# Last stage of an attention, slot-routing and squared-ReLU kernel: half 0 of the next g made in a row, products of w_in moved later in the step

## The chip, the cores and the metric

The kernel runs on one core of a Trainium2 chip. The metric is the device time of one execution in microseconds (us), lower is better. Engines are named as in the profile: PE (TensorE), with PEld for its weight loads, ACT (ScalarE), DVE (VectorE), POOL (GpSimd), SP (SyncE, which issues the transfers). Every engine executes its own instructions in the order in which they were written; between engines only semaphores order the work.

## What is computed

Three layers follow one another. The first two are not touched by the change; the third is where it lies.

```python
x = attention(q, k, v)            # 4 x 8 heads, 576 positions, window of 128; x is [2304, 512]
logits = x @ phi                  # soft routing to 8 experts of 4 slots
d = softmax over tokens;  c = softmax over slots
slot_out = relu((d.T @ x)[e] @ w1[e]) @ w2[e]      # 32 slots, 512 wide
x = c @ slot_out                  # [2304, 512], rank 32
h = maximum(x @ w_in, 0)          # w_in [512, 2048]
out = (h * h) @ w_out             # w_out [2048, 512]
```

Since x has rank 32, the kernel multiplies w_in by the 32 slots first (a small matrix M, 16 blocks of 128 columns) and then gets h from M and the routing weights c.

## The kernel before, in words

The last stage walks over 48 **units** (tb, f): tb is one of three blocks of 768 tokens, f one of 16 blocks of 128 hidden columns, in three groups of f (0 to 2, 3 to 7, 8 to 15), for each group all three tb. For one unit, `emit_h` makes h (two matmuls of 384 columns into the PSUM banks "xb" and "B", half 0 and half 1); `emit_relu` (ACT) reads each half into a buffer; `emit_sq` squares it in float32, `emit_hi` squares it once more with rounding to the matmul type, `emit_lo` (DVE) subtracts the two. High and low part together are "g". `emit_g(i, s)`, s from 0 to 5, takes one sixth of unit i's tokens: three matmuls of 512 columns into one PSUM bank. s of 0 to 2 read half 0 of g, s of 3 to 5 half 1. In the last f of a group each `emit_g` also empties its bank (L741 on ACT and L743 on DVE in the first group, L745 or L749 on DVE in the others).

The weights w_in and w_out arrive as 64-bit floats and are converted in the same stage, block by block: `conv1` on POOL (two operations of L601), `conv2` on DVE (L615, L617, L619 for each half: half 0 is w_in and gives `cin`, half 1 is w_out and gives `co`), `conv3` (ACT L633, then a subtraction L634). `emit_M1` (PE L640, ACT L642) and `emit_M2` (PE L646, ACT L648, DVE L649) turn `cin` into block f of M. M1 uses the bank "xb" and M2 the bank "B", the banks of h.

A prologue written out by hand does unit 0 and the conversions of the first blocks. Then a loop of **steps** i = 1 to 47 emits the matmuls of unit i and, among them, everything that makes g of unit i + 1, together with half a conversion (`half_at[i]` names block and half; where the half is 1 the step also has M1, M2 and `conv3`: an **M step** below). Order within an engine is the order of these calls; the loop body before is:

```python
emit_g(i, 0); hb = emit_h(i + 1); emit_relu(i + 1, hb); emit_g(i, 1)
emit_M1(fm, "xb"); emit_sq(i + 1, ...); emit_g(i, 2); emit_M2(fm, "B")
emit_hi(i + 1); emit_lo(i + 1, 0, dve); emit_lo(i + 1, 1, dve)
conv2(ch[0], halves=((ch[1],),)); conv3(fm, dve)
emit_g(i, 3); emit_g(i, 4); emit_g(i, 5)
```

Of the kernel before, what the change touches and what calls it, by code (L numbers as in the profile page):

```python
# [27 lines left out]
def attn_moe_relu2_kernel(ctx: ExitStack, tc: tile.TileContext, z0, q, k, v, vr, phi, w1, w2, w_in, w_out, cst, out):  # L28
    nc = tc.nc
    pe, act, dve, pool, sp = nc.tensor, nc.scalar, nc.vector, nc.gpsimd, nc.sync  # L30
# [9 lines left out]
    def bank(tag, name):  # L40
        return psum[0].tile([128, 512], F32, tag=tag, name=name, bufs=NBUF[tag])
# [41 lines left out]
    def take(shape, dt, name):  # L83
        used[0] += 1
        assert used[0] <= RING
        return ring.tile(shape, dt, tag="w", name=name)

    def pump(free, spare):
        used[0] -= free
        while wq and used[0] < RING - spare:  # L90
            load_next_w()
# [495 lines left out]
    def temp(tag, i, n, w, dt):  # L587
        if tag not in arena:
            arena[tag] = take([128, 2048], dt, f"arena_{tag}")
        i %= n  # L590
        return arena[tag][:, w * i:w * i + w]

    def spare():
        return 5 - len(arena) + 3 - len(psto) + min(2, 8 - made[0])

    def conv1(f):

        t = wt["f", f]
        y = temp("y", f, 2, 1024, I32).rearrange("p (a n) -> p a n", a=2)
        for a in range(2):  # L600
            pool.tensor_scalar(out=y[:, a].bitcast(F32), in0=t[:, a, :, 1].bitcast(F32), scalar1=2.0 ** -112, scalar2=0.0, op0=ALU.mult, op1=ALU.add)  # L601
        yz_t[f] = y

    def conv2(f, hooks=(), halves=((0, 1),)):
        t, y = wt["f", f], yz_t[f]
        if f not in cin:
            cin[f] = temp("cin", f, 4, 512, F32)
            co_t[f] = temp("co", f, 4, 512, F32)
        dst = (cin[f], co_t[f])
        hooks = dict(hooks)  # L610
        for n, a in enumerate(halves):
            for k in range(3):
                for h in a:
                    if k == 0:
                        dve.tensor_scalar(out=y[:, h], in0=y[:, h], scalar1=3, scalar2=0x7FFFFFFF, op0=ALU.logical_shift_left, op1=ALU.bitwise_and)  # L615
                    elif k == 1:
                        dve.scalar_tensor_tensor(out=y[:, h], in0=t[:, h, :, 1], scalar=-0x80000000, in1=y[:, h], op0=ALU.bitwise_and, op1=ALU.bitwise_or)  # L617
                    else:
                        dve.scalar_tensor_tensor(out=dst[h].bitcast(I32), in0=t[:, h, :, 0], scalar=29, in1=y[:, h], op0=ALU.logical_shift_right, op1=ALU.bitwise_or)  # L619
                if (n, k) in hooks:  # L620
                    hooks[n, k]()
        if 1 in halves[-1]:
            wt.pop(("f", f))
            yz_t.pop(f)
            pump(1, spare())

    def conv3(f, eng=pool):
        p = f // 2
        if f % 2 == 0:
            whl[p] = take([128, 2, 2, 512], F32R, "whl")  # L630
            made[0] += 1
        t, c = whl[p], co_t.pop(f)
        act.activation(out=t[:, f % 2, 0], in_=c, func=AF.Copy)  # L633
        eng.tensor_tensor(out=t[:, f % 2, 1], in0=c, in1=t[:, f % 2, 0].bitcast(F32), op=ALU.subtract)  # L634
# [39 lines left out]
    NF = DFF // 128  # L674
# [7 lines left out]
    def emit_h(i):  # L682
        tb, f = units[i]
        hb = []
        for hf in range(2):
            hb.append(bank(("xb", "B")[hf], "h"))
            c0 = TB * tb + HB * hf
            pe.matmul(out=hb[hf][:, 0:HB], lhsT=Mst[:, 128 * f:128 * f + 128], rhs=cst_sb[:, c0:c0 + HB], start=True, stop=True)  # L688
        return hb
# [3 lines left out]
    def emit_relu(i, hb, hfs=(0, 1), cl=slice(0, HB)):  # L693
        if i not in g_t:
            k0 = [(2 * i + hf) % 4 for hf in range(2)]
            g = [hT_flat[:, HB * k:HB * k + HB] for k in k0]
            g_t[i] = [temp("gh%d" % (k // 2), k % 2, 2, 2 * HB, F32R).rearrange("p (a n) -> p a n", a=2) for k in k0]
            lo_t[i] = (g, g_t[i])
        for hf in hfs:
            act.activation(out=rbuf[hf][:, cl], in_=hb[hf][:, cl], func=AF.Relu)  # L700

    def emit_sq(i, eng, hfs=(0, 1), cl=slice(0, HB)):
        g = lo_t[i][0]
        for hf in hfs:
            r = rbuf[hf][:, cl]
            if eng is act:
                act.activation(out=g[hf][:, cl], in_=r, func=AF.Square)  # L707
            else:
                eng.tensor_tensor(out=g[hf][:, cl], in0=r, in1=r, op=ALU.mult)  # L709

    def emit_hi(i, hfs=(0, 1), cl=slice(0, HB)):
        for hf in hfs:
            act.activation(out=lo_t[i][1][hf][:, 0, cl], in_=rbuf[hf][:, cl], func=AF.Square)  # L713

    def emit_lo(i, hf, eng, cl=slice(0, HB)):
        g, gh = lo_t[i]
        eng.tensor_tensor(out=gh[hf][:, 1, cl], in0=g[hf][:, cl], in1=gh[hf][:, 0, cl].bitcast(F32), op=ALU.subtract)  # L717
# [5 lines left out]
    def emit_g(i, s):  # L723
        tb, f = units[i]
        if f in firsts:
            acc_t[s] = bank(atags[s], "acc")
        gh = g_t[i][s // 3]
        c0 = 128 * (s % 3)
        w = whl[f // 2]
        for a, (x, y) in enumerate(((0, 0), (1, 0), (0, 1))):  # L730
            pe.matmul(out=acc_t[s], lhsT=gh[:, x, c0:c0 + 128], rhs=w[:, f % 2, y, :], start=(f in firsts and a == 0), stop=(f in lasts and a == 2))  # L731
        if f not in lasts:
            return
        a = acc_t.pop(s)
        r0, k = TB * tb + 128 * s, 6 * tb + s
        if f == GROUPS[0][-1]:
            if k >= 6 and k % 4 == 2:
                psto.append(take([128, 4, 512], F32, "psum"))
                part.extend(psto[-1][:, j] for j in range(4))
            if s % 2:  # L740
                act.activation(out=part[k], in_=a, func=AF.Copy)  # L741
            else:
                dve.tensor_copy(out=part[k], in_=a)  # L743
        elif f != NF - 1:
            dve.tensor_tensor(out=part[k], in0=a, in1=part[k], op=ALU.add)  # L745
        else:
            cls = (slice(0, 512),) if i < len(units) - 1 or s < 5 else (slice(0, 256), slice(256, 512))
            for cl, eng in zip(cls, (sp, act)):
                dve.tensor_tensor(out=part[k][:, cl], in0=a[:, cl], in1=part[k][:, cl], op=ALU.add)  # L749
                eng.dma_start(out=out[r0:r0 + 128, cl], in_=part[k][:, cl])  # L750
# [6 lines left out]
    hb = emit_h(0)  # L757
# [23 lines left out]
    hb = emit_h(1)  # L781
# [11 lines left out]
    emit_lo(1, 1, pool)  # L793
    emit_g(0, 5)
    emit_M2(2, "B")
    conv1(4)
    conv2(3, halves=((0,),))
    conv3(2)
    g_t.pop(0)

    halves = [(3, 1)] + [(f, a) for f in range(4, NF) for a in range(2)]
    steps = [i for i in range(1, len(units)) if not (units[i][1] in lasts and i > 8)]
    half_at = dict(zip(steps, halves))
    conv1_at = {i - 1: f for i, (f, a) in half_at.items() if a == 0 and f > 4}
    last_conv = max(half_at)
    where = {u: i for i, u in enumerate(units)}
    assert all(i < where[0, f] for i, (f, a) in half_at.items())
    for i in range(1, len(units)):
        tb, f = units[i]
        nxt = i + 1 < len(units)  # L810
        ch = half_at.get(i)
        fm = ch[0] if ch and ch[1] == 1 else None
        if i in conv1_at:
            conv1(conv1_at[i])
        emit_g(i, 0)
        hb = emit_h(i + 1) if nxt else None
        if nxt:
            emit_relu(i + 1, hb)
        emit_g(i, 1)
        if fm is not None:  # L820
            emit_M1(fm, "xb")
        if nxt:
            emit_sq(i + 1, act if i <= last_conv else dve)
        emit_g(i, 2)
        if fm is not None:
            emit_M2(fm, "B")
        if nxt:
            emit_hi(i + 1)
            emit_lo(i + 1, 0, dve)
            emit_lo(i + 1, 1, dve)  # L830
        if ch:
            conv2(ch[0], halves=((ch[1],),))
        if fm is not None:
            conv3(fm, dve)
        for s in range(3, 6):
            emit_g(i, s)
        g_t.pop(i)
        if tb == NT // TB - 1 and f % 2 and f < NF - 1:
            whl.pop(f // 2)
            pump(1, spare())  # L840
# [49 lines left out]
```

## Time and profile before

| | us |
|---|---|
| median of 3 runs (441.91 to 443.17) | 442.53 |
| the profiled execution, as timed | 442.01 |
| its span, first to last instruction | 440.2 |
| from h of unit 2 to h of unit 31 (steps 1 to 29) | 156.11 |
| the last matmuls, after that | 76.03 |

Read it so: the span is 1.8 us shorter than the time of the same execution. The stretch in the fourth line is the part of the last stage that still converts weights; in the fifth nothing is left but h, g and the output.

### The profile page before, as it was taken

To read this page: it belongs to the slowest core of one execution; us is meant where nothing else is said; L and a number is where in the kernel's file an instruction comes from. 1 tells how busy PE (TensorE), PEld (TensorE's weight loads), DVE (VectorE), ACT (ScalarE), POOL (GpSimd) and SP (SyncE) were. 2 spreads that over 40 slices of the span, in tenths; PEclk is the share of its full clock that TensorE was granted. 3 is DMA by queue.
4 is the path that set the end of the run, shared out by engine and by line. 5 is a ranking of instruction groups with operands and counts; after the bars stand their busy time and mean duration, and the time that the engine had idled before them with its cause. 6 is when DMAs were issued, how large, how long until landed. Compare 5 with 4: busy or idle time off the path is not lost. (4 is left out here: it accounts for less than half of the span.)

```text
span 440.2 us, 8019 instructions
## 1 busy us (share of the span) xinstructions
PE 417.0 (95%) x2623; PEld 306.9 (70%) x2623; DVE 290.2 (66%) x962; ACT 239.0 (54%) x759; POOL 91.3 (21%) x189
## 2 busy tenths in 40 slices
PE   6999999999999999978998999999999999999995
PEld 5777768768766533456776677777777788888884
DVE  4877867877866446586775767566686666447444
ACT  4877857867866211354666655565555553434340
POOL 3544435433532010455111111110100000000000
PEclk9999999999999999968999999999999999999999
DMA  7979859856778799995200502020000003003003
GB/s 233 295 284 270 286 201 279 281 167 235 245 244 322 269 413 424 408 410 228 95 2 0 191 1 96 1 98 0 1 0 1 1 25 121 0 0 144 0 1 144
DMA packets 36794, 70.62 MB, mean 160 GB/s; under 512 B 19984, under 2 KB 22160, under 8 KB 32656
## 3 DMA queue, kind: packets, MB, share of 16 engines
q1 hardware_dynamic: 36608, 69.97, 44.9%
q8 instruction: 21, 0.34, 0.3%
q14 instruction: 21, 0.17, 0.1%
q10 hardware_dynamic: 144, 0.13, 0.1%
HBM read 65.37 MB, written 4.72 MB: 159 GB/s over the span
## 5 line engine op out<-in xcount | busy, mean ns | idle before, releaser
L731 PE MATMUL acc<-whl,arena_gh 128*128 128x512 f32 x864 | 222.2, 403 | 4.3 <-DVE arena_gh L717 1.9
L731 PEld LDWEIGHTS acc<-whl,arena_gh 128*128 128x128 f32 x864 | 160.2, 191 | 43.8 <-DVE arena_gh L717 8.5
L188 POOL TENSOR_SCALAR p<-p,st 128x192 f32<-128x192 f32 (+1 forms) x142 | 56.6, 412 | 79.6 <-DVE st L184 24.7
L176 ACT ACTIVATE p<-p,st 128x192 f32<-128x192 f32 (+1 forms) x144 | 61.2, 428 | 6.3 <-DVE st L166 6.3
L159 PE MATMUL s<-kt,zq 128*128 128x192 f32 (+2 forms) x288 | 60.2, 335 | 4.1 <-DMA kt<-in_k_dram 3.4
L700 ACT ACTIVATE acc<-h 128x384 f32<-128x384 f32 (+2 forms) x49 | 23.6, 481 | 66.6 <-PE h L688 33.6
L717 DVE TENSOR_TENSOR arena_gh<-hT,arena_gh 128x384 fp32r<-128x384 f32 (+1 forms) x95 | 48.6, 551 | 15.8 <-ACT arena_gh L713 12.9
L159 PEld LDWEIGHTS s<-kt,zq 128*128 128x128 f32 x288 | 45.5, 198 | 8.9 <-DMA zq<-in_z_dram 4.1
L601 POOL TENSOR_SCALAR arena_y<-f 128x512 f32<-128x512 f32 x32 | 23.0, 724 | 133.8 <-DVE arena_co L619 62.6
L166 DVE CUSTOM_DVE_ANT_0 p<-s,tbl 128x192 f32<-128x192 f32 (+1 forms) x144 | 41.8, 326 | 5.2 <-PE s L159 4.6
L229 DVE COPY ptb<-tq 64x128 f32<-64x128 f32 x128 | 35.3, 280 | 9.4 <-PE tq L209 7.4
L227 ACT ACTIVATE ptb<-tp 128x256 f32<-128x256 f32 (+1 forms) x72 | 25.5, 355 | 14.7 <-PE tp L207 14.5
L709 DVE TENSOR_TENSOR hT<-acc 128x384 f32<-128x384 f32 (+1 forms) x19 | 10.7, 565 | 29.8 <-ACT acc L700 29.8
L633 ACT ACTIVATE whl<-arena_co 128x512 fp32r<-128x512 f32 x16 | 10.1, 632 | 32.7 <-DVE arena_co L619 22.5
L246 PE MATMUL xa<-ptb,vt 128*64 128x256 f32 x192 | 27.6, 396 | 0.0
L176 ACT ACTIVATION_READ_ACCUMULATOR p<-p,st 128x1 f32 x144 | 27.4, 190 | 0.0
L207 PE MATMUL tp<-cs,p 128*128 128x128 f32 x128 | 26.1, 275 | 1.0 <-ACT xT L263 1.0
L688 PE MATMUL h<-cst_sb,Mst 128*128 128x384 f32 x96 | 25.1, 343 | 0.7 <-DVE Mst L649 0.6
L713 ACT ACTIVATE arena_gh<-acc 128x384 fp32r<-128x384 f32 (+2 forms) x49 | 25.3, 516 | 0.1
L617 DVE SCALAR_TENSOR_TENSOR arena_y<-f,arena_y 128x512 int32<-128x512 int32 x32 | 24.5, 765 | 1.1
L713 ACT ACTIVATE arena_gh<-hT 128x384 fp32r<-128x384 f32 x48 | 25.0, 521 | 0.0
L700 ACT ACTIVATE hT<-h 128x384 f32<-128x384 f32 x48 | 23.3, 485 | 0.0
(172 smaller groups left out, 488.7 us busy)
## 6 DMA issues: line engine op xcount, KB each, us to landing
w_w<-in_w_dram SPq DMA_DIRECT2D x32, 1024.0 KB, 6.7
f<-in_w_in_dram SPq DMA_DIRECT2D x16, 512.0 KB, 10.2
f<-in_w_out_dram SPq DMA_DIRECT2D x16, 512.0 KB, 10.2
zq<-in_q_dram SPq DMA_DIRECT2D x30, 144.0 KB, 3.8
kt<-in_k_dram SPq DMA_DIRECT2D x15, 288.0 KB, 4.1
vt<-in_v_dram SPq DMA_DIRECT2D x16, 256.0 KB, 6.5
out_dram<-psum SPq DMA_DIRECT2D x11, 256.0 KB, 2.1
out_dram<-xn_all SPq DMA_DIRECT2D x4, 256.0 KB, 2.0
```

The costliest lines, as they stand in the source:

```text
L159: pe.matmul(out=sb_t[t][:, 256 * i:256 * i + n], lhsT=zq[u % NQ][:, c].rearrange("p a b -> p (a b)"), rhs=kt_t[u][:, 64 * c + 64 - n:64 * ...
L166: dve.tensor_tensor_reduce(out=p, in0=sb_t[t][:, 256 * i:256 * i + n], in1=tbl[:, 192 * pr + 192 - n:192 * pr + 192], scale=-0.125, scalar ...
L176: act.activation(out=p, in_=p, func=AF.Exp, bias=st[:, i:i + 1], scale=-1.0, accum_out=st[:, 2 + i:3 + i])
L188: eng.tensor_scalar(out=p, in0=p, scalar1=st[:, 4 + i:5 + i], scalar2=0.0, op0=ALU.mult, op1=ALU.add)
L207: pe.transpose(A[:, i, :], p, ident)
L227: act.activation(out=dst, in_=src, func=AF.Copy)
L229: dve.tensor_copy(out=dst, in_=src)
L246: pe.matmul(out=xa_t[u][po:po + 64, 128 * j:128 * j + 256], lhsT=v_t[u][:, j, po:po + 64], rhs=pt[:, 0:4, po:po + 64], start=(j == 0), sto ...
L700: act.activation(out=rbuf[hf][:, cl], in_=hb[hf][:, cl], func=AF.Relu)
L713: act.activation(out=lo_t[i][1][hf][:, 0, cl], in_=rbuf[hf][:, cl], func=AF.Square)
L717: eng.tensor_tensor(out=gh[hf][:, 1, cl], in0=g[hf][:, cl], in1=gh[hf][:, 0, cl].bitcast(F32), op=ALU.subtract)
L731: pe.matmul(out=acc_t[s], lhsT=gh[:, x, c0:c0 + 128], rhs=w[:, f % 2, y, :], start=(f in firsts and a == 0), stop=(f in lasts and a == 2))
```

## The change

The first conversions of the prologue for block 3 move into the loop: half 0 of block 3 in step 1, half 1 in step 2, and so on: each later half moves on by one of the steps that have a conversion. There are 13 M steps as before, the first now step 2 (it was 1) and the last step 29 (it was 28). `conv3(2)` subtracts on DVE instead of POOL. Within a step, relu, square and rounded square of half 0 stand in a row on ACT, and those of half 1 after them; on DVE the order becomes low part 0, conversion, low part 1, L649, L634. M1 stands after `emit_g(i, 2)` and M2 after `emit_g(i, 4)`.

```diff
@@ -793,47 +793,51 @@
     emit_lo(1, 1, pool)
     emit_g(0, 5)
     emit_M2(2, "B")
-    conv1(4)
-    conv2(3, halves=((0,),))
-    conv3(2)
+    conv3(2, dve)
     g_t.pop(0)
 
-    halves = [(3, 1)] + [(f, a) for f in range(4, NF) for a in range(2)]
+    halves = [(f, a) for f in range(3, NF) for a in range(2)]
     steps = [i for i in range(1, len(units)) if not (units[i][1] in lasts and i > 8)]
     half_at = dict(zip(steps, halves))
-    conv1_at = {i - 1: f for i, (f, a) in half_at.items() if a == 0 and f > 4}
+    conv1_at = {i - 1: f for i, (f, a) in half_at.items() if a == 0 and f > 3}
     last_conv = max(half_at)
     where = {u: i for i, u in enumerate(units)}
-    assert all(i < where[0, f] for i, (f, a) in half_at.items())
+    assert all(i + 2 <= where[0, f] for i, (f, a) in half_at.items())
     for i in range(1, len(units)):
         tb, f = units[i]
         nxt = i + 1 < len(units)
         ch = half_at.get(i)
         fm = ch[0] if ch and ch[1] == 1 else None
+        sq = act if i <= last_conv else dve
         if i in conv1_at:
             conv1(conv1_at[i])
         emit_g(i, 0)
-        hb = emit_h(i + 1) if nxt else None
         if nxt:
-            emit_relu(i + 1, hb)
+            hb = emit_h(i + 1)
+            emit_relu(i + 1, hb, (0,))
+            emit_sq(i + 1, sq, (0,))
+            emit_hi(i + 1, (0,))
+            emit_lo(i + 1, 0, dve)
         emit_g(i, 1)
+        emit_g(i, 2)
+        if nxt:
+            emit_relu(i + 1, hb, (1,))
         if fm is not None:
             emit_M1(fm, "xb")
         if nxt:
-            emit_sq(i + 1, act if i <= last_conv else dve)
-        emit_g(i, 2)
+            emit_sq(i + 1, sq, (1,))
+            emit_hi(i + 1, (1,))
+        if ch:
+            conv2(ch[0], halves=((ch[1],),))
+        if nxt:
+            emit_lo(i + 1, 1, dve)
+        emit_g(i, 3)
+        emit_g(i, 4)
         if fm is not None:
             emit_M2(fm, "B")
-        if nxt:
-            emit_hi(i + 1)
-            emit_lo(i + 1, 0, dve)
-            emit_lo(i + 1, 1, dve)
-        if ch:
-            conv2(ch[0], halves=((ch[1],),))
+        emit_g(i, 5)
         if fm is not None:
             conv3(fm, dve)
-        for s in range(3, 6):
-            emit_g(i, s)
         g_t.pop(i)
```

## Rows read from the trace of the kernel before

**Rows 1.** The profile's page, parts 1 and 2: busy time and share of the span of each engine, and the clock granted to TensorE in 40 equal slices (9 is full speed).
```profile
PE 417.0 (95%) x2623; PEld 306.9 (70%) x2623; DVE 290.2 (66%) x962; ACT 239.0 (54%) x759; POOL 91.3 (21%) x189
PEclk9999999999999999968999999999999999999999
```

**Rows 2.** Stretches of the span, each from the start of h of one unit to the start of h of another: us of the stretch, then busy us (and instructions) of PE, PEld, DVE, ACT, POOL, then the granted clock, the share of the transfer engines and GB/s. In order: steps 1, 11, 12, 13, 14, 24 and 33, and last steps 1 to 29 together.
```profile
199.86:208.55 8.69, 6.98 (x30) 5.38 (x31) 5.51 (x9) 3.36 (x9) 4.62 (x5) 0.80 0.53 207
...
257.98:263.93 5.95, 5.38 (x31) 4.06 (x30) 3.68 (x8) 3.07 (x8) 0.66 (x1) 1.00 0.01 3
263.93:268.81 4.88, 4.78 (x21) 3.65 (x20) 2.79 (x6) 3.04 (x7) 0.66 (x1) 1.00 0.59 196
268.81:273.46 4.65, 4.65 (x21) 3.65 (x20) 4.55 (x9) 2.52 (x6) 0.67 (x1) 1.00 0.06 22
273.46:278.74 5.28, 5.28 (x31) 4.03 (x30) 3.74 (x8) 3.05 (x8) 0.00 (x0) 1.00 0.00 0
...
324.63:329.91 5.28, 5.28 (x31) 4.03 (x30) 3.74 (x8) 3.06 (x8) 0.00 (x0) 1.00 0.00 0
...
369.47:373.92 4.45, 4.45 (x22) 3.73 (x21) 1.97 (x4) 1.70 (x4) 0.00 (x0) 1.00 0.00 0
...
199.86:355.97 156.11, 147.36 (x710) 112.42 (x711) 105.97 (x191) 90.83 (x221) 18.54 (x26) 0.99 0.13 46
```

**Rows 3.** The waits of PE and of PEld in steps 1 to 29: engine, tile and line, what it waited for, us in total, times, longest.
```profile
PE MX L640 <- DVE arena_cin L619: 6.8, 10, 1.7
...
PEld acc L731 <- DVE arena_gh L717: 5.8, 15, 0.4
```

**Rows 4.** Timeline of PE in step 11 (an M step): start, us, engine and line, operation, count, and in brackets the idle time before it with its releaser. The twelve matmuls of the last row are s of 3 to 5 of this step and s = 0 of the next. The matmuls' ends are modelled, so the starts are read.
```profile
257.98 0.51 PE L688 MATMUL h<-cst_sb,Mst 128*128 128x384 f32 x2
258.33 0.86 PE L731 MATMUL acc<-whl,arena_gh 128*128 128x512 f32 x3
259.76 0.42 PE L640 MATMUL MX<-arena_cin,soT 128*32 128x128 f32 x8 [0.56 <-DVE arena_cin L619]
260.12 0.98 PE L731 MATMUL acc<-whl,arena_gh 128*128 128x512 f32 x3
260.93 0.38 PE L646 MATMUL MY<-ms,cs 128*128 128x128 f32 x2
261.07 3.02 PE L731 MATMUL acc<-whl,arena_gh 128*128 128x512 f32 x12
```

**Rows 5.** Timeline of ACT: first two operations of the prologue, the second of which reads what the first wrote; then from steps 11 and 12 (the conversion L633 is issued in step 11 and stands ahead of step 12's relu).
```profile
195.20 0.49 ACT L700 ACTIVATE acc<-h 128x384 f32<-128x384 f32 x1 [0.80 <-PE h L688]
195.72 0.52 ACT L713 ACTIVATE arena_gh<-acc 128x384 fp32r<-128x384 f32 x1
...
258.42 0.49 ACT L700 ACTIVATE acc<-h 128x384 f32<-128x384 f32 x1 [1.24 <-PE h L688]
...
261.35 0.28 ACT L648 ACTIVATE Mst<-MY 128x128 fp32r<-128x128 f32 x1
...
264.97 0.63 ACT L633 ACTIVATE whl<-arena_co 128x512 fp32r<-128x512 f32 x1 [2.52 <-issue]
265.51 0.47 ACT L700 ACTIVATE acc<-h 128x384 f32<-128x384 f32 x1
...
267.08 0.52 ACT L713 ACTIVATE arena_gh<-acc 128x384 fp32r<-128x384 f32 x1
267.50 0.52 ACT L713 ACTIVATE arena_gh<-hT 128x384 fp32r<-128x384 f32 x1
```

**Rows 6.** Timeline of DVE: one emptying of a bank in step 6, then step 11.
```profile
232.47 0.69 DVE L743 COPY psum<-acc 128x512 f32<-128x512 f32 x1
...
261.66 0.29 DVE L649 TENSOR_TENSOR Mst<-MY,Mst 64x128 fp32r<-64x128 f32 x1 [2.05 <-ACT Mst L648]
262.07 1.03 DVE L717 TENSOR_TENSOR arena_gh<-hT,arena_gh 128x384 fp32r<-128x384 f32 x2
263.02 0.42 DVE L615 TENSOR_SCALAR arena_y<-arena_y 128x512 int32<-128x512 int32 x1
263.48 0.69 DVE L617 SCALAR_TENSOR_TENSOR arena_y<-f,arena_y 128x512 int32<-128x512 int32 x1
264.20 0.69 DVE L619 SCALAR_TENSOR_TENSOR arena_co<-f,arena_y 128x512 int32<-128x512 int32 x1
```

**Rows 7.** Around step 1: a stretch behind its M1 (columns as in rows 2), then timelines of PE, DVE and POOL; the last row is POOL in step 12.
```profile
203.20:206.50 3.30, 3.30 (x13) 2.69 (x10) 0.73 (x2) 2.20 (x6) 1.28 (x2) 0.50 0.35 133
...
202.87 0.43 PE L640 MATMUL MX<-arena_cin,soT 128*32 128x128 f32 x8 [1.71 <-DVE arena_cin L619]
...
194.97 1.65 DVE L617 SCALAR_TENSOR_TENSOR arena_y<-f,arena_y 128x512 int32<-128x512 int32 x1
...
199.83 0.80 DVE L615 TENSOR_SCALAR arena_y<-arena_y 128x512 int32<-128x512 int32 x1
200.67 1.02 DVE L617 SCALAR_TENSOR_TENSOR arena_y<-f,arena_y 128x512 int32<-128x512 int32 x1
201.72 1.01 DVE L619 SCALAR_TENSOR_TENSOR arena_cin<-f,arena_y 128x512 int32<-128x512 int32 x1
...
200.31 1.87 POOL L601 TENSOR_SCALAR arena_y<-f 128x512 f32<-128x512 f32 x2
...
264.97 0.66 POOL L601 TENSOR_SCALAR arena_y<-f 128x512 f32<-128x512 f32 x1 [4.62 <-DVE arena_co L619]
```

## The prediction, made before the result was known

> **What bounds the kernel now.** I read the page first: PE is busy for 95% of the span at nearly full clock, DVE and ACT for much less [rows 1]. So only time in which PE stands, or does the same work at the lower clock, can be won. Next the stretches between the starts of h in consecutive steps [rows 2]. A step that has only h and 18 matmuls takes 4.45 us, and PE has no hole in it: that is the floor. With M1 and M2 and without a wait it takes 5.28 us (steps 14 and 24), so M1 and M2 cost 0.83. But step 11, also an M step, takes 5.95, step 12 4.88 though it has no M1, and step 1 8.69. Steps 1 to 29 take 156.11 us; after them the steps are at the floor, so the change can win nothing there.
>
> The waits name two causes [rows 3]. M1 stands 6.8 us in 10 M steps for `cin`, which DVE converts last. In step 11 the three matmuls of s = 1 start at 258.33 and need 0.68, yet M1 starts at 259.76 [rows 4]. And the weight loads of `emit_g` wait for low parts of g. Why these are late is seen on ACT: in step 12 relu of half 0 starts at 265.51 instead of 0.44 after h (as in step 11, 257.98 to 258.42), because L633 stands ahead of it and itself waits for `co` [rows 4, 5]. The relus, squares and rounded squares of both halves must then all pass before DVE takes low part 0.
>
> Step 1 has both troubles and a third: M1 waits 1.71 us for `cin` of block 3, whose conversions take 0.80, 1.02 and 1.01, and in the stretch behind that wait the granted clock is 0.50, the 1.2 GHz level [rows 7].
>
> **The change, part by part.** I lay one new M step out from its h start (0), with pitches from rows [rows 4 to 6].
>
> *ACT.* Relu 0 at 0.44. Square 0 reads what relu wrote: such a pair is 0.52 apart (195.20 to 195.72), so 0.96. Rounded square 0 follows by 0.42 at 1.38 and ends at 1.90. Relu 1 starts at 1.80. M1 starts behind two groups of 0.68 and h (0.35), at 1.72 plus a small gap, and its copy on ACT is done by about 2.6; square 1 and rounded square 1 end by about 3.6.
>
> *DVE.* Low part 0 starts at 1.90. Two low parts take 0.95 to the next operation, one 0.48: L615 at 2.38, L617 0.46 later at 2.84, L619 0.72 later at 3.56, ending at 4.25. Low part 1 starts at 4.25 and ends at 4.80; L649 starts at 4.73 and ends at 5.02. L634 follows when L633 is done, about 5.7, which is 0.4 into the next step, before that step's low part 0.
>
> *What each consumer needs.* Low part 0 ends at 2.45; s = 0 of the next unit starts at 4.45 - 0.68 = 3.77 or later, so that wait goes, with 1.3 to spare. Low part 1 is needed at 4.45 + 0.35 + 1.37 = 6.17: 1.37 to spare. `cin` is made a step earlier, so M1's wait goes. L633 stands behind rounded square 1 and finds `co` at 4.3, so it ends about 5.0 and the next relu (5.28 + 0.44) is not held. M2's copy on ACT ends before low part 1 does, as M2 to copy takes 0.42.
>
> *The new wait.* L649 reads bank "B", into which half 1 of the next h goes. In an M step of 5.28 that matmul starts at 5.28 + 0.17 = 5.45; L649 ends at 5.02, so 0.43 to spare. In steps 2 and 8 two DVE copies of a bank (s = 2 and 4, 0.69 each) stand ahead of L649 as well: 5.02 + 1.38 = 6.40, a stall of 0.95 each. Behind it stand all later matmuls.
>
> *Cost of M1 and M2 in the new place.* Not shown. From below the gaps from their own start to the next group: 0.36 (259.76 to 260.12) and 0.14 (260.93 to 261.07), 0.50. From above 0.83 as measured. Nothing in the move shortens the switch from and to small matmuls, so I take 0.83.
>
> *Prologue, POOL and DMA.* The first L615 to L619 of block 3 leave the place in front of M1; `conv3(2)` goes to DVE, where an L634 (about 0.7) fits before low part 0 of step 1, 1.90 after h. I cost it at nothing; uncovered it would be those 0.7, once. POOL's first conversion of a block is released as soon as an earlier block's half is done [rows 7], steps before it is used, and stays so. The transfers of w_in and w_out are issued when a block is consumed, with several blocks in the ring, so the shift by a step costs nothing; a late one would hold only POOL. Step 1, without M1 and its wait, then runs at full clock; if the 3.3 us at the lower level stayed, that would add 1.65, as half of it would be lost.
>
> *Emptying at the end of a group.* Step 13, with six of them, takes 4.65, 0.20 over the floor. Between 0 and 0.20 for each of six such steps (2, 5, 8, 13, 18, 23); low part 0 no longer waits behind three of them, so 0.10.
>
> **The sum for steps 1 to 29.** 29 x 4.45 = 129.05; 13 x 0.83 = 10.79; 2 x 0.95 = 1.90; 6 x 0.10 = 0.60; together 142.3. Against 156.11 the gain is 13.8. The profiled execution took 442.01, so 428.2. The median of the runs is 0.5 higher; I forecast 428.5, between the two readings. With M1 and M2 at 0.50 and no stalls the sum is 135.55, gain 20.6: 421.5.
>
> **A rule weighed against a row.** Beside POOL's L601, two of which took 1.87 instead of 2 x 0.66, L615, L617 and L619 took 0.80, 1.02 and 1.01 instead of 0.42, 0.69 and 0.69: both engines got slower, DVE by 1.03 in all [rows 6, 7]. POOL's L601 is released by the end of L619 [rows 7], so in the new order it falls beside low part 1 and L649, where before DVE was idle or done.
>
> The Trainium skill, "SBUF — State Buffer", section "Who interferes with whom", says that DVE and GpSimd contend only for one shared pair of ports, held exclusively for a whole instruction. By that rule the loser would stand still for all of the other's operation; the rows agree that there is contention, but show both longer.
>
> **Rivals.**
> *POOL blocks DVE once per M step.* If low part 1 or L649 stood for a whole L601, 0.66, L649 would end at 5.68, half 1 of h would wait 0.23, and 13 of these cost 3.0: 431.5. For it: the overlap is new. Against: low part 1 has started before L601 is released.
>
> *Conversions stretched as in step 1.* L615 to L619 1.03 longer in every step puts L649 at 6.05; h waits 0.60 in 13 M steps, 7.8: 436. Against: from step 2 on the operations take 0.42, 0.69 and 0.69, since POOL's part comes after them.
>
> *The gap only moves; no change.* Low part 1, now behind the conversion, could hold s = 3 of the next unit. To give back 13.8 in 29 steps it must cost 0.48 each, so be 1.37 + 0.48 = 1.85 later than laid out: 442.5. Against: the worst stretch of a whole conversion in rows is 1.03.
>
> *Slower: L649 holds h.* Its place is bank "B" in every M step. It decides from a delay of 0.43 + 13.8 / 13 = 1.5 us beyond my layout. For it: one L617 beside POOL took 1.65 instead of 0.69, 2.4 times [rows 7]. Were all three stretched so (1.80 to 4.3), L649 would be 2.5 late, the stall 2.1, 13 times 27: 455. Against: that row is from the prologue, beside several POOL operations in a row.
>
> **How the numbers follow.** Forecast 0.64, POOL's blocking 0.11, stretched conversions 0.10, no change 0.07, slower 0.08. Faster 0.85, the same 0.07 (within 0.3%, 1.3 us, about what a measurement of this kernel can tell from no change), slower 0.08. The range runs from the lower bound, 421.5, to the stretched conversions, 436, and leaves out the last two cases and part of the spread about the others.
>
> **What the profile after would show.** The wait of M1 for `cin` gone; the weight loads' wait for low parts near zero; steps without M1 at 4.45 and M steps near 5.28; steps 1 and 2 together about 9.7 where step 1 alone took 8.69, with the clock at 1.00; L633 no longer ahead of relu 0; a new wait of h for L649 of steps 2 and 8. I am wrong if h waits for L649 in all M steps, if low part 1 holds s = 3, or if M steps cost far from 0.83.

## The result, and the profile after

| | before | after |
|---|---|---|
| median of the runs, us | 442.85 (4 runs, 441.91 to 443.52) | 428.85 (4 runs, 428.07 to 429.97) |
| the profiled execution, as timed | 442.01 | 429.43 |
| its span | 440.2 | 427.6 |
| h of unit 2 to h of unit 31 | 156.11 | 141.74 |

The ratio is 0.9687, 95% interval 0.9655 to 0.9719: 14 us faster. The forecast was 428.5.

First the page of the kernel after, parts 1 and 2:

```profile
PE 410.1 (96%) x2623; PEld 306.1 (72%) x2623; DVE 292.7 (68%) x961; ACT 248.7 (58%) x761; POOL 95.0 (22%) x188
PEclk9999999999999999987999999999999999999999
```

Against [rows 1] the same number of matmuls takes 7 us less of PE's busy time. The page alone does not say where the gain is; the stretches from h to h do. The columns are those of [rows 2]; the rows are steps 1, 2, 3, 11, 12 and 13 of the kernel after, and steps 1 to 29 together:

```profile
201.90:206.45 4.55, 4.55 (x21) 3.83 (x21) 3.22 (x6) 3.03 (x7) 2.27 (x4) 1.00 0.97 383
206.45:211.72 5.27, 5.27 (x31) 4.03 (x30) 4.31 (x9) 4.47 (x11) 1.17 (x2) 1.00 0.07 26
211.72:217.10 5.38, 4.72 (x21) 3.66 (x20) 4.35 (x9) 3.27 (x8) 1.42 (x2) 1.00 0.54 195
...
252.49:256.94 4.45, 4.45 (x22) 3.72 (x21) 2.99 (x6) 2.75 (x6) 0.16 (x1) 1.00 0.01 4
256.94:262.21 5.27, 5.27 (x31) 4.03 (x30) 3.50 (x8) 3.77 (x9) 1.63 (x2) 1.00 0.03 5
262.21:266.66 4.45, 4.45 (x21) 3.72 (x20) 3.74 (x7) 2.75 (x6) 0.00 (x0) 1.00 0.66 231
...
201.90:343.64 141.74, 140.42 (x710) 111.99 (x711) 104.51 (x190) 96.70 (x223) 21.94 (x25) 1.00 0.14 51
```

Of the 14.37 us that this stretch got shorter, 7.43 are time in which PE stood (156.11 less 147.36 before, 141.74 less 140.42 after). The other 6.94 had been counted as busy: 1.70 in step 1, the lower clock (6.98 against 5.28 for an M step), and most of the rest in steps like step 12 before, where PE is counted busy for 4.78 [rows 2] with what takes 4.45 when no weight load waits. So a share of busy time of 95% hides a part of what can be won; steps laid beside the floor do not.

The work of DVE, 104.51, is about what it was (105.97), and ACT has 6 us more; PE waits for them in two places only. What is left of waits of PE and PEld in the same stretch, columns as in [rows 3] (the list has beside these only waits of PEld on "issue", for which the profile shows no releaser: 4.6 us at M1 and 2.6 us at `emit_g`):

```profile
PE h L688 <- DVE Mst L649: 1.3, 2, 0.7
...
PEld h L688 <- DVE Mst L649: 2.6, 3, 1.0
```

M1's wait for `cin` and the wait for low parts are gone, and the new wait is the one that was expected, twice. Here it is at the end of step 2 (h start 206.45), on DVE and PE:

```profile
211.65 0.68 DVE L743 COPY siT<-acc 128x512 f32<-128x512 f32 x1
212.37 0.29 DVE L649 TENSOR_TENSOR Mst<-MY,Mst 64x128 fp32r<-64x128 f32 x1
...
212.72 0.44 PE L688 MATMUL h<-cst_sb,Mst 128*128 128x384 f32 x1 [0.66 <-DVE Mst L649]
213.00 4.27 PE L731 MATMUL acc<-whl,arena_gh 128*128 128x512 f32 x18
```

Now step 12, an M step in the new order, on ACT, DVE and POOL, and the next h on PE (its second matmul is 0.17 behind the start shown):

```profile
257.31 0.49 ACT L700 ACTIVATE acc<-h 128x384 f32<-128x384 f32 x1 [1.65 <-PE h L688]
257.83 0.52 ACT L707 ACTIVATE hT<-acc 128x384 f32<-128x384 f32 x1
258.26 0.51 ACT L713 ACTIVATE arena_gh<-acc 128x384 fp32r<-128x384 f32 x1
258.68 0.47 ACT L700 ACTIVATE hT<-h 128x384 f32<-128x384 f32 x1
...
258.81 0.56 DVE L717 TENSOR_TENSOR arena_gh<-hT,arena_gh 128x384 fp32r<-128x384 f32 x1 [1.64 <-ACT arena_gh L713]
259.28 0.42 DVE L615 TENSOR_SCALAR arena_y<-arena_y 128x512 int32<-128x512 int32 x1
...
261.07 0.55 DVE L717 TENSOR_TENSOR arena_gh<-hT,arena_gh 128x384 fp32r<-128x384 f32 x1
...
261.24 0.90 POOL L601 TENSOR_SCALAR arena_y<-f 128x512 f32<-128x512 f32 x1 [3.56 <-DVE arena_co L619]
...
261.65 0.29 DVE L649 TENSOR_TENSOR Mst<-MY,Mst 64x128 fp32r<-64x128 f32 x1
...
262.21 0.50 PE L688 MATMUL h<-cst_sb,Mst 128*128 128x384 f32 x2
```

Counted from its h start, 256.94: relu 0 at 0.37, square 0.89, rounded square 1.32, relu 1 at 1.74, low part 0 at 1.87, L615 at 2.34, low part 1 at 4.13, L649 from 4.71 to 5.00; the next h at 5.27, its half 1 at 5.44. The reader sees 0.44 us between the end of L649 and the matmul that needs its bank. POOL's L601 starts 0.17 behind low part 1 and takes 0.90 where it took 0.66 [rows 7]; low part 1 takes its 0.55.

### The profile page after: what moved, and what is told of

Its sections match the earlier page's. It is cut to its first block, busy times and chain, and to the rows that moved or that the text cites. A ratio compares the mean times of both kernels' runs of the same rounds, so it can differ in the third digit from the quotient of the medians.

```text
span 427.6 us, 7977 instructions
## 1 busy us (share of the span) xinstructions
PE 410.1 (96%) x2623; PEld 306.1 (72%) x2623; DVE 292.7 (68%) x961; ACT 248.7 (58%) x761; POOL 95.0 (22%) x188
## 4 chain that ended last, share of the span: by engine, by line
PE 51%; DVE 2%; ACT 1%; issue 0%; DVEq 0%
PE acc L731 45%; PE h L688 4%; PE MX L640 1%; DVE psum L749 1%; PE MY L646 1%; DVE arena_y L617 1%; DVE arena_y L615 0%; ACT whl L633 0%; DVE arena_gh L717 0%; DVE Mst L649 0%; DVE arena_co L619 0%; ACT siT L741 0%; ACT psum L741 0%; DVEq L890 0%; ACT ms L642 0%
## 5 line engine op out<-in xcount | busy, mean ns | idle before, releaser
L731 PE MATMUL acc<-whl,arena_gh 128*128 128x512 f32 x864 | 214.9, 397 | 2.4 <-DVE arena_gh L717 1.9
L717 DVE TENSOR_TENSOR arena_gh<-hT,arena_gh 128x384 fp32r<-128x384 f32 (+1 forms) x95 | 52.7, 555 | 38.5 <-ACT arena_gh L713 34.1
L601 POOL TENSOR_SCALAR arena_y<-f 128x512 f32<-128x512 f32 x32 | 28.4, 892 | 122.3 <-DVE arena_cin L619 55.1
L688 PEld LDWEIGHTS h<-cst_sb,Mst 128*128 128x128 f32 x96 | 18.2, 191 | 7.7 <-DVE Mst L649 3.8
```

## The experiments

The theory: the gain is PE's holes in all steps, closed by getting DVE to the conversion and to L649 early; what remains is the floor, 0.83 for each M step, and the time by which L649 is late for the next h. The rivals: it is the start with its wait and low clock; it is the late products alone; it is the order of the halves alone. Four kernels take the change apart.

**e1: the start alone**, on the kernel before:

```diff
-    conv1(4)
-    conv2(3, halves=((0,),))
-    conv3(2)
+    conv3(2, dve)
...
-    halves = [(3, 1)] + [(f, a) for f in range(4, NF) for a in range(2)]
+    halves = [(f, a) for f in range(3, NF) for a in range(2)]
...
```

> Only the start of the change: conversions of block 3 leave the prologue, every later half one step on, conv3(2) on DVE; the loop body stays the old one. Theory (PE's holes in all steps are the gain): step 1 falls from 8.69 to an M-less step of about 4.9, step 29 becomes an M step of about 5.95, so the gain is about 2.7 us: 440, and M1 still waits about 6 us in all for cin. Rival (the start with its low clock is most of the gain): 431 to 434.

Measured: 442.15 against 442.81, ratio 0.998 (0.9962 to 0.9998). Steps 1, 12, 13 and 1 to 29, then ACT at the start of step 13 (h start 267.58):

```profile
201.17:205.73 4.56, 4.56 (x20) 3.85 (x21) 2.62 (x5) 2.81 (x7) 2.19 (x3) 1.00 0.94 370
261.63:267.58 5.95, 5.38 (x32) 4.06 (x30) 3.69 (x8) 3.07 (x8) 0.65 (x1) 1.00 0.00 0
267.58:272.98 5.40, 4.78 (x21) 3.65 (x20) 4.59 (x9) 3.04 (x7) 0.67 (x1) 1.00 0.53 193
201.17:356.14 154.97, 145.71 (x711) 111.38 (x711) 103.30 (x188) 91.02 (x222) 16.69 (x25) 1.00 0.13 46
...
268.62 0.63 ACT L633 ACTIVATE whl<-arena_co 128x512 fp32r<-128x512 f32 x1 [2.52 <-issue]
269.16 0.48 ACT L700 ACTIVATE acc<-h 128x384 f32<-128x384 f32 x1
```

Step 1 falls by 4.13, and the granted clock of the stretch is 1.00. But 1.1 us remain in steps 1 to 29, less than half of the 2.7 that I had expected. With every half a step later, the steps that empty the banks (13, 18, 23) now follow M steps, have L633 ahead of their relu, and take 5.37 to 5.43 (step 13: 5.40, not 4.65 [rows 2]). The old loop gives back most of what the start wins. The rival that the start is most of the gain falls.

**e2: the start and the late products, g in the old order:**

```diff
         emit_g(i, 1)
+        emit_g(i, 2)
         if fm is not None:
             emit_M1(fm, "xb")
         if nxt:
             emit_sq(i + 1, act if i <= last_conv else dve)
-        emit_g(i, 2)
-        if fm is not None:
-            emit_M2(fm, "B")
...
+        emit_g(i, 3)
+        emit_g(i, 4)
+        if fm is not None:
+            emit_M2(fm, "B")
+        emit_g(i, 5)
...
```

> The start and the new places of M1 (after s = 2) and M2 (after s = 4), but g in the old order, both halves together and the conversion behind both low parts. Theory: M1's wait goes, but L649 stands behind both low parts and the conversion, at about 6.6 to 6.9 us into an M step, and half 1 of the next h waits about 1.5 us in 13 M steps; 442 to 448, slower than with the start alone. Rival (the late products are the gain by themselves, M1's 6.8 us of waiting): 433 to 434.

Measured: 452.70, ratio 1.022 (1.0171 to 1.0269): 10 us slower than before, and above the 442 to 448 that I had expected. The end of an M step on PE and on DVE:

```profile
222.01 0.33 PE L688 MATMUL h<-cst_sb,Mst 128*128 128x384 f32 x1
223.79 0.44 PE L688 MATMUL h<-cst_sb,Mst 128*128 128x384 f32 x1 [1.45 <-DVE Mst L649]
...
220.59 1.03 DVE L717 TENSOR_TENSOR arena_gh<-hT,arena_gh 128x384 fp32r<-128x384 f32 x2 [3.18 <-PE acc L731]
...
223.44 0.29 DVE L649 TENSOR_TENSOR Mst<-MY,Mst 64x128 fp32r<-64x128 f32 x1
```

Half 0 of h starts at 222.01, half 1 only at 223.79, when L649 has let bank "B" go. The step after an M step takes 6.16, 1.71 over the floor, where I had expected about 1.5; M1's own waiting is gone, as in the whole change. So the late products by themselves are a loss: this is the slower rival of the prediction, made by an order of DVE's work instead of by POOL.

**e3: the start and the new order, products in their old places:**

```diff
         emit_g(i, 1)
-        emit_g(i, 2)
         if nxt:
             emit_relu(i + 1, hb, (1,))
         if fm is not None:
             emit_M1(fm, "xb")
+        emit_g(i, 2)
+        if fm is not None:
+            emit_M2(fm, "B")
...
         emit_g(i, 4)
-        if fm is not None:
-            emit_M2(fm, "B")
```

> The start and the new order of g, but M1 after s = 1 and M2 after s = 2 as before (relu of half 1 stands ahead of M1, for its bank). Theory: M2 comes 0.4 us too early for the copy of M1, which stands behind relu 1 on ACT at 2.2 to 2.5; 13 x 0.4 lost against the whole change, while L649 is early and the two stalls of h in steps 2 and 8 go (1.6 to 1.9 back): about 432. M1 itself waits for nothing. Rival (the places of M1 and M2 are worth half the gain or more): 436 or above.

Measured: 430.54, ratio 0.9726 (0.9705 to 0.9747); steps 1 to 29 in 143.98. An ordinary M step, on PE and ACT:

```profile
217.21 0.96 PE L731 MATMUL acc<-whl,arena_gh 128*128 128x512 f32 x3
218.15 0.49 PE L646 MATMUL MY<-ms,cs 128*128 128x128 f32 x2
...
217.83 0.27 ACT L642 ACTIVATE ms<-MX 128x128 f32<-128x128 f32 x1
```

M2 starts 0.94 behind a group that needs 0.68, when M1's copy is done. Eleven of the M steps take 5.50 to 5.55, 0.22 to 0.27 over 5.28 and not the 0.4 expected. Steps 3 and 9 are at 4.45, since L649 is early, but steps 2 and 8 take 5.99 and 6.04: there a copy of a bank on ACT (in step 2 at 207.02, for 0.58) stands ahead of relu 1 and of M1's copy, and M2 stands 0.47 for that. So most of the two stalls moved and did not go. The order brings 11.0 of the 14.4 us (154.97 in e1 to 143.98), and the places of the products, on top of it, the last 2.2.

**e4: the new loop with the old start.**

```diff
-    conv3(2, dve)
+    conv1(4)
+    conv2(3, halves=((0,),))
+    conv3(2)
...
-    halves = [(f, a) for f in range(3, NF) for a in range(2)]
+    halves = [(3, 1)] + [(f, a) for f in range(4, NF) for a in range(2)]
...
```

> The new loop body with the old start (half 0 of block 3 converted in the prologue, conv3(2) on POOL). Theory: M1 of step 1 waits about 1.15 us for cin; if the granted clock falls behind it as before, another 1.7: 430.0 to 431.7. Rival (the start is worth nothing, since the wait in step 1 is hidden by the new order): 428.9.

Measured: 428.54, ratio 0.968 (0.9662 to 0.9699). M1 of step 1, then steps 1 and 1 to 29:

```profile
203.61 0.43 PE L640 MATMUL MX<-arena_cin,soT 128*32 128x128 f32 x8 [1.03 <-DVE arena_cin L619]
...
200.58:207.08 6.50, 5.46 (x30) 4.17 (x31) 6.36 (x7) 3.48 (x9) 4.96 (x5) 1.00 0.68 267
...
200.58:343.51 142.93, 140.53 (x710) 112.04 (x711) 107.91 (x191) 96.34 (x221) 23.84 (x26) 1.00 0.13 50
```

M1 waits about as expected (1.03, not 1.15), and the stretch is 1.19 longer than in the whole change (141.74), yet the granted clock stays 1.00. In the time of the runs the 1.2 us cannot be seen: the intervals overlap, and the start of step 1 alone lies anywhere from 199.86 to 201.90 in these profiles. So the start is worth about 1.2 us by the trace and nothing that the runs can tell: the time is the rival's 428.9 and not the 430.0 to 431.7 of the theory, although the wait is not hidden.

The next four are the whole change with one thing altered. Beside them the whole change was run again: 429.74, ratio 0.9697 (0.9672 to 0.9723), steps 1 to 29 in 141.81.

> The whole change again, as the measure for the three kernels beside it: 428.5 to 429.5, steps 1 to 29 in about 141.7 us.

**e6: L649 made late.** Low part 1 is made three times in M steps.

```diff
-            emit_lo(i + 1, 1, dve)
+            for _ in range(3 if fm is not None else 1):
+                emit_lo(i + 1, 1, dve)
```

> The whole change, with low part 1 made three times over in M steps (the same values), so that L649 comes 0.96 us later. Theory (0.43 us to spare at bank B): h waits 0.53 in 11 M steps and 0.96 more in steps 2 and 8, 7.7 us in all: 436.5. Rival (the layout is hidden with much more room, since h could be late without holding PE): no more than 1 us, 429.5.

Measured: 443.81, ratio 1.0032 (1.0011 to 1.0053), steps 1 to 29 in 157.92: the whole gain is lost by one subtraction that comes late. One M step (h start 251.77):

```profile
255.91 2.07 DVE L717 TENSOR_TENSOR arena_gh<-hT,arena_gh 128x384 fp32r<-128x384 f32 x3
258.01 0.29 DVE L649 TENSOR_TENSOR Mst<-MY,Mst 64x128 fp32r<-64x128 f32 x1
...
257.05 0.33 PE L688 MATMUL h<-cst_sb,Mst 128*128 128x384 f32 x1
258.36 0.44 PE L688 MATMUL h<-cst_sb,Mst 128*128 128x384 f32 x1 [0.98 <-DVE Mst L649]
```

My delay was mis-sized: the three low parts take 2.07, so L649 comes 1.52 later, not 0.96. The account of the bank holds: 1.52 - 0.43 = 1.09 expected with that delay, and the step after an M step takes 5.69, 1.24 over the floor. The rival of much more room falls. The room that counts is 1.52 - 1.24 = 0.28: half 1 starts 0.06 after L649's end, and the next group follows it by 0.28 instead of 0.17.

Where the 1.52 come from is seen in the second of these three low parts by itself, in POOL's operation of the same step, and in M step 27, beside which POOL has nothing left to convert:

```profile
256.50 0.89 DVE L717 TENSOR_TENSOR arena_gh<-hT,arena_gh 128x384 fp32r<-128x384 f32 x1
...
256.08 0.90 POOL L601 TENSOR_SCALAR arena_y<-f 128x512 f32<-128x512 f32 x1 [4.79 <-DVE arena_co L619]
...
346.08 1.74 DVE L717 TENSOR_TENSOR arena_gh<-hT,arena_gh 128x384 fp32r<-128x384 f32 x3
```

The second low part starts while L601 runs and takes 0.89; the first and the third take 0.55 and 0.56. In steps 27 and 29, with no L601 beside them, all three take 0.55 or 0.56 and start 0.59 apart, 1.74 and 1.73 in all. So two more low parts delay L649 by 1.19, and POOL's operation adds the other 0.33. The step after step 27 takes 5.36, 0.91 over the floor: 1.19 - 0.91 = 0.28, the same room with another delay.

**e7: the conversion behind low part 1.**

```diff
+        if nxt:
+            emit_lo(i + 1, 1, dve)
         if ch:
             conv2(ch[0], halves=((ch[1],),))
-        if nxt:
-            emit_lo(i + 1, 1, dve)
```

> The whole change, with the conversion behind low part 1 instead of ahead of it. Theory (what matters is how early DVE gets to the conversion and so to L649): L649 ends at about 6.1 us into an M step, h waits 0.7 in 11 M steps and 1.8 to 2.0 in steps 2 and 8, so 9 to 10 us more: 438 to 439. Rival (half 0 first is the whole of it, the place of the conversion is free): 428.9.

Measured: 440.09, ratio 0.9937 (0.9918 to 0.9957), steps 1 to 29 in 152.64, 10.8 more, where I had expected 9 to 10. L649 and the next h:

```profile
255.90 0.29 DVE L649 TENSOR_TENSOR Mst<-MY,Mst 64x128 fp32r<-64x128 f32 x1
...
255.35 0.33 PE L688 MATMUL h<-cst_sb,Mst 128*128 128x384 f32 x1
256.25 0.44 PE L688 MATMUL h<-cst_sb,Mst 128*128 128x384 f32 x1 [0.57 <-DVE Mst L649]
```

The step after an M step takes 5.28, 0.83 over the floor. With the late products, half 0 first is thus worth little (2.3 us under the 154.97 of e1) if DVE then waits for half 1 before it converts: the conversion has to fill the time between the low parts.

**e5 and e8: a better version.** What is left over the floor and the M steps are the two waits for L649 in steps 2 and 8, behind copies of a bank. e5 issues M2 earlier there and gives the copy of s = 2 to ACT:

```diff
...
-            if s % 2:
+            if s in (1, 2, 5):
                 act.activation(out=part[k], in_=a, func=AF.Copy)
...
+        early = i in (2, 8)
-        emit_g(i, 3)
+        emit_g(i, 3, (lambda: emit_M2(fm, "B")) if early else None)
...
```

> The whole change, but in steps 2 and 8 M2 is issued between the matmuls and the emptying of s = 3, and of the copies of a bank ACT takes s = 1, 2 and 5, DVE s = 0, 3 and 4, so that no copy stands ahead of L649. Theory (h waits for L649 behind two copies): L649 ends near 5.0 us into steps 2 and 8 as in the other M steps, steps 3 and 9 fall from 5.38 to 4.45, 1.8 us less in steps 1 to 29, about 427. Rival (h waits there for something else, such as the rounds of the PSUM banks at the end of a group): no change, 428.9.

Measured: 427.51, ratio 0.9649 (0.9629 to 0.967), steps 1 to 29 in 140.96, 0.85 less than beside it and not 1.8. Step 8:

```profile
238.31 0.49 PE L646 MATMUL MY<-ms,cs 128*128 128x128 f32 x2 [0.28 <-ACT ms L642]
...
236.64 1.07 ACT L743 ACTIVATE psum<-acc 128x512 f32<-128x512 f32 x2
237.59 0.49 ACT L700 ACTIVATE hT<-h 128x384 f32<-128x384 f32 x1
237.96 0.29 ACT L642 ACTIVATE ms<-MX 128x128 f32<-128x128 f32 x1
```

Steps 3 and 9 are at 4.45, but two copies on ACT now stand ahead of relu 1 and of M1's copy, and M2 waits for that: steps 2 and 8 take 5.80. e8 puts these copies off until their place is free:

```diff
...
+        wait = i in (2, 8)
-        emit_g(i, 1)
-        emit_g(i, 2)
+        emit_g(i, 1, not wait)
+        emit_g(i, 2, not wait)
...
             emit_hi(i + 1, (1,))
+        if wait:
+            emit_empty(i, 1, act)
+            emit_empty(i, 2, act)
...
-        emit_g(i, 3)
-        emit_g(i, 4)
+        emit_g(i, 3, not wait)
+        emit_g(i, 4, not wait)
         if fm is not None:
             emit_M2(fm, "B")
+        if wait:
+            emit_empty(i, 3, dve)
+            emit_empty(i, 4, dve)
```

(`emit_empty` is the copy out of a bank taken out of `emit_g`.)

> The whole change with M1 and M2 where it has them; in steps 2 and 8 the copies of s = 1 and 2 go to ACT behind rounded square 1, those of s = 3 and 4 to DVE behind L649. Theory: L649 ends at about 5.0 us into these steps and M2 waits for nothing, so steps 2 and 8 take 5.28 and steps 3 and 9 take 4.45: steps 1 to 29 in about 139.9 us, 1.8 less than the whole change: 427. Rival (the copies put off now hold a bank or the relu behind them, and h or a group waits instead): steps 1 to 29 in 141 or more.

> The whole change, as the measure for the kernel beside it: 428.5 to 430, steps 1 to 29 in 141.8 us.

Measured: 426.06, ratio 0.9646 (0.962 to 0.9672); the whole change beside it 428.75, ratio 0.9696 (0.9674 to 0.9717). Steps 1 to 29 and L649 of step 2 (h start 204.97):

```profile
200.39:340.31 139.92, 139.92 (x711) 112.11 (x712) 104.65 (x190) 96.89 (x223) 21.91 (x25) 1.00 0.15 54
...
209.69 0.30 DVE L649 TENSOR_TENSOR Mst<-MY,Mst 64x128 fp32r<-64x128 f32 x1
210.02 0.69 DVE L746 COPY xn_all<-acc 128x512 f32<-128x512 f32 x1
```

L649 ends at 5.02, the copies follow it, and PE is busy for all of the stretch, as expected to 0.1 us. The two intervals only just miss each other and single runs overlap (425.19 to 428.53 against 428.21 to 429.43), but the trace shows the 1.8 us where they were foretold.

## Why the prediction was right, point by point

- *The floor.* 29 steps at 4.45: held. Step 1, 4.55, is the only one over it by as much as 0.1 without a stall named.
- *M1 and M2 at 0.83.* M steps take 5.27 or 5.28. The lower end, 0.50, played no part; the switch to and from the small matmuls did not shrink in the new place.
- *The layout of an M step.* Forecast, and in brackets measured: low part 0 at 1.90 (1.87), low part 1 at 4.25 (4.13), L649 ending at 5.02 (5.00). Pitches read from rows of the old order hold in the new one, the pair of dependent ACT operations (0.52) included.
- *The stall in steps 2 and 8.* 0.95 each forecast; steps 3 and 9 take 5.38, 0.93 over the floor. e8 shows the cause by removing it. That the size came out so close is luck: two errors cancel. The two copies delay L649 by 1.21 and not by 1.38, so it ends 6.21 into step 2 (212.66) and not at 6.40; but half 1 starts 0.06 after that end, and the next group 0.28 behind it instead of 0.17, a cost of 0.17 that the sum did not have.
- *Emptying at the end of a group.* 0.10 for each of six steps forecast; 0.00 measured: step 13 takes 4.45, as do 5, 18 and 23, and steps 2 and 8 take 5.27. This term, 0.6 us, is nearly all of the difference between 142.3 and 141.74.
- *The start.* Steps 1 and 2 take 9.82 together (9.7 forecast), at full clock. But the first waits there are worth less than they look: with the old start the new loop is only 1.2 us longer, and e4 waits 1.03 us for `cin` without a fall of the clock. Why the clock fell in the kernel before, after a wait of 1.71 [rows 7], and not in e4 is left open. It need not fall in every run of that kernel. All twelve profiles have a stretch of 3 to 7 us at the lower level in the prologue, between 189 and 198 us, and only that of the kernel before has a second one, in step 1. Its runs have mean granted clocks from 0.984 to 0.995; at 0.994 PE loses about 440 x 0.006 = 2.6 us (an estimate), less than the 5 us that the stretches of 6.8 and 3.3 us cost in this profile. So up to 1.65 of the 156.11 that the forecast started from belongs to this one execution.
- *Outside the stretch.* I had it unchanged. In the two profiles the way to step 1 is 2.04 longer, in code that the change does not touch, and the other profiles spread over the same range; the part behind step 29 is 0.3 shorter. The span gained 14.37 - 2.04 + 0.27 = 12.6, and the medians of the runs differ by 14.0. So the steps are forecast to 0.6 us, but that the time of the runs, 428.85, lies within 0.4 of 428.5 is closer than one profile could promise.
- *POOL beside DVE.* The overlap is there, but it is POOL that gets longer (0.66 to 0.90), and low part 1, which started first, keeps its 0.55; L649, beside the same L601, keeps its 0.29. In e6 the order is turned round for one operation: the second low part starts behind L601 and takes 0.89 instead of 0.56. By the rule of the Trainium skill, "SBUF — State Buffer", section "Who interferes with whom", the one that issues first holds the shared ports and the other stands; these rows agree with that on who gets longer. On how much they do not quite agree: the second gets 0.24 and 0.33 longer, where 0.38 and 0.48 of the first were left. Neither rival built on POOL came true: low part 1 starts ahead of L601, and L649 behind it is not held.
- *What the prediction did not say.* That the parts win little or lose when alone. The start and the late products without the order cost 10 us (e2), the start without the order wins 1 (e1). My own expectations of e1 and e6 were off because I counted one effect of an edit and not the next: in e1 L633 ahead of steps 13, 18 and 23, in e6 the time between subtractions that write over each other, and POOL's operation beside them.

## What to carry to other kernels

Find the engine that must not stand, write down when each of its next operations needs what the others make, and lay the others' queues out against those times with pitches from the trace; here that gave the new step to 0.1 us. The same edit can win or lose by a single small operation in a queue: the 0.29 us subtraction that frees a bank belongs ahead of everything that nobody is waiting for. When a product is moved later, look at what it frees as well as at what it needs.

## What the runs showed of the hardware that was not expected

Of a DVE subtraction and a POOL operation that overlap, the one that started second got longer: L601 0.90 instead of 0.66 behind low part 1, and a low part 0.89 instead of 0.56 behind L601 (e6). The total of 2.07 for three low parts, 0.76 from one to the next on average, hides this; without POOL they start 0.59 apart (e6, steps 27 and 29), where two that write different tiles start 0.48 apart [rows 6]. And a matmul that had to wait for its bank lets the next group start 0.28 behind it instead of 0.17, so a stall costs about 0.1 more than the wait itself.
